# Products with v on four quarters of the array, two banks per product, in an attention + feed-forward kernel

## The chip, the cores and the metric

The kernel runs on one core of a Trainium2 chip. The metric is the device time of one execution in microseconds (us). TensorE (PE) multiplies matrices and writes to PSUM banks; VectorE (DVE) and ScalarE (ACT) work on data in SBUF and PSUM; GpSimd (POOL) works on SBUF alone; SyncE (SP) issues the DMAs. The engines run their instructions in program order and wait for each other by semaphores.

## The reference

Attention over a window of 128 positions for 8 batches of 8 heads (576 positions, 64 values a head), and behind it two big products with a nonlinear step between them:

```python
scores = scale * np.matmul(q, k.transpose(0, 1, 3, 2))
mask = (rel >= 0) & (rel < window)
scores = np.where(mask, scores + bias[None], -1000000000.0)
attn = np.exp(scores - max) / (sum + 1e-09)
x = np.matmul(attn, v)             # 4608 tokens x 512 after reordering
h = x @ w_in                       # 512 -> 2048
g = h * erf(softplus(h))
return g @ w_out                   # 2048 -> 512
```

## The kernel before

**Attention** is cut into 48 spans, numbered n = 0 to 47: twelve chunks c of 384 tokens, and for each of them four pairs g of heads (j = 0, 1 in a pair). Two of three chunks are of a first kind (`w` = 0, one batch, 32 spans in all); the third is of a second kind (`w` = 1, the rest of two batches, 16 spans). Each span runs through these steps:

- `scores`: 64x64 matmuls q k^T into two PSUM banks, one for each head j. Head j lies on partitions 64 j and up, so it uses one half of the array's rows; the two halves of the queries use one half of its columns each. A matmul uses one quarter of the array. In the second kind the three tiles are done as a group of two and a group of one.
- `softmax`: DVE adds the bias table and takes the minimum (line 470), ACT takes the exponentials (line 478).
- `normalise`: DVE inverts the sums; POOL (in the first four spans also DVE) scales the probabilities p (line 501).
- `transpose_bank`: PE transposes p by blocks of 128 (line 521) into a bank `t`, and DVE or ACT copies it to `pa`, two or three banks for each span. After the transpose the two heads lie beside each other.
- `av`: px = v^T p^T on the whole array (line 537), 6 matmuls of 64 to 192 columns in the first kind and 10 in the second, all into one bank. v lies in memory with zeros for the other head, so that the two heads don't mix. From span 8 on px shares the bank `t` with the transposes.
- DVE or ACT copies px to `xs` (or, in the first two chunks, straight to `xr`), and SP stores it.

**The feed-forward part** takes x by chunks. Everything is done in split precision: a value is held as a high and a low part, and each product is three matmuls. Line 732 makes h, line 714 or 718 (ACT or DVE) copies it out, lines 769 and 771 are softplus and erf on ACT, lines 781 and 785 are DVE's, and line 803 makes o. The first pass does 7 of the 16 slices of w_in and w_out for all tokens (h blocks of 384 columns) and runs interleaved with attention; the second pass does the other 9 (blocks of 512) and begins when attention has ended and its SBUF is free. Each slice of the weights is prepared by ACT and DVE (lines 608 to 629).

**Order.** Nothing is reordered on the chip. `Plan.run` lists all steps with the buffers that they read and write and their planned costs, and places them one after another: on each free engine the ready step with the smallest due time `at` goes first, if its buffers are free. A step that lists several engines takes the one that can have it first. Pools give the number of buffers: banks `s` 2, `t` 1, `h` 2, three for o; `TB`, `PB`, `VB` are those of pa, p and v. In the first 8 spans (`SPARE`) the banks of o and h, not yet in use, serve attention too.

Of the kernel before, what the change touches and what calls it, by code (L numbers as in the profile page):

```python
# [18 lines left out]
NPAIR = H // 2  # L19
# [21 lines left out]
MB, KH, KS = 15, 4, 2  # L41
PB, XB, OB, TB = 8, 3, 3, 4
QB, VB = 4, 2
# [15 lines left out]
TILES = [  # L59
    [(2, 128), (3, 0), (3, 0)],  # L60
    [(3, 0), (3, 0), (3, 0)],
]
QUERIES = [(128, 0, 640), (0, 128, 256)]
PIECES = [[(128, 384)], [(0, 128), (384, 512)], [(512, 768)]]
KEYS = [
# [6 lines left out]
]  # L72
GROUPS = [[(0, 1, 2)], [(0, 1), (2,)]]
BANKS = [
# [5 lines left out]
]  # L80
VALUES = [
# [6 lines left out]
]  # L88
SUB = ALU.subtract

# [251 lines left out]
class Attention:  # L342


    def __init__(self, tc, plan, ctx, actx, qk, vb, bias, ident, moe):
# [26 lines left out]
        self.step = self.n = 0  # L372
        self.loaded = []
        for c in range(3 * B // 2):
            for g in range(NPAIR):
                self.span(c, g)
                self.n += 1

# [26 lines left out]
    def values(self, c, g, w, at):  # L405

        v = Buf(self.vp, [P, 10, P], F32, "v", VB, f"v{self.n}")
        blocks = 10 if w else 6
        self.plan.op(emit=lambda e: self.nc.sync.dma_start(v[:, :blocks], self.src_v[c, g, :, :blocks]), w=[v], at=at,
                     **dma(P * blocks * P * 4))  # L410
        return v
# [9 lines left out]
    def scores(self, w, x, ready, at):  # L421
# [5 lines left out]
        for group in groups:  # L427
# [31 lines left out]
    def softmax(self, g, w, t, ps, low, total, at):  # L459
        nc, op = self.nc, self.plan.op  # L460
        blocks, c0 = TILES[w][t]
        n = 64 * blocks
        nm = f"{self.n}_{t}"
        pt = Buf(self.pp, [P, 3, 2, 64], F32, "p", PB, f"p{nm}")
        cut = lambda x: x.rearrange("p (c d) -> p c d", d=64)
        table = self.tables[g]

        def biased(e):
            for j in range(2):
                nc.vector.tensor_tensor_reduce(  # L470
                    out=pt[:, :blocks, j, :], in0=cut(ps[j].all), in1=cut(table.ap[:, j * 256 + c0 : j * 256 + c0 + n]),
                    scale=-0.125, scalar=3.0e38, op0=ALU.add, op1=ALU.min, accum_out=low[:, j : j + 1],
                )
# [9 lines left out]
        return pt  # L483

    def normalise(self, w, p, st, totals, at):
# [9 lines left out]
        for t in range(3):  # L495
            blocks = TILES[w][t][0]

            def scaled(e, t=t, blocks=blocks):
                for j in range(2):
                    dst = p[t][:, :blocks, j, :]  # L500
                    (nc.vector if e == "DVE" else nc.gpsimd).tensor_scalar(  # L501
# [7 lines left out]
    def transpose_bank(self, w, bi, p, sb, at):  # L509
        nc, op = self.nc, self.plan.op  # L510
        parts, c0, c1 = BANKS[w][bi]
        nm = f"t{self.n}_{bi}"
# [5 lines left out]
        def transposes(e):  # L518
            cut = ps[:, :].rearrange("p (c d) -> p c d", d=64)
            for n, (t, kb, a, b) in enumerate(parts):  # L520
# [7 lines left out]
        op({"DVE": dve(c1 - c0), "Act": act(c1 - c0, src=0.06)},  # L528
           lambda e: self.copy(e, sb[bi][:, : c1 - c0], ps[:, c0:c1]), r=[ps], w=[sb[bi]], at=at)

    def av(self, w, step, dst, v, sb, at):
        todo = VALUES[w][step]
        last = step == len(VALUES[w]) - 1
# [8 lines left out]
        self.plan.op({"PE": sum(fp32_us(x[-1]) for x in todo) + 0.015}, products,  # L542
                     r=[v, *(sb[x] for x in sorted({y[1] for y in todo}))], w=[dst], at=at)

    def span(self, c, g):
        op, n = self.plan.op, self.n
        w = int(c % 3 == 2)
# [6 lines left out]
        for t in range(3):  # L554
# [4 lines left out]
            self.step += 1  # L559
        self.normalise(w, p, st, totals, at)  # L560
        at += LT
        sb = [Buf(self.ptp, [P, 512], F32, "pa", TB, f"pa{n}_{x}") for x in range(len(BANKS[w]))]
        for bi in range(len(BANKS[w])):
            self.transpose_bank(w, bi, p, sb, at)
# [12 lines left out]
        self.moe.x_parts[c].append(xd)  # L577
        op(emit=lambda e: self.nc.sync.dma_start(xd.all, xs.all), r=[xs], w=[xd],
           at=at + 0.1, **dma(P * CH * 4))
# [312 lines left out]
def _layout(q, k, v, moe_w_in, moe_w_out):  # L892
# [7 lines left out]
    qk = np.zeros((nc, NPAIR, 2, D, 1024), q.dtype)  # L900
    vb = np.zeros((nc, NPAIR, 2, 64, 10, 2, D), v.dtype)
    for c in range(nc):
# [5 lines left out]
        else:  # L908
            order = [(qh, x, 6), (qh, x, 7), (qh, y, 6), (qh, y, 7), (qh, x, 8), (qh, y, 8)]
            order += [(kh, b, n) for b in (x, y) for n in range(4, 9)]  # L910
            values = [(b, kb) for b in (x, y) for kb in range(4, 9)]
        for n, (src, b, block) in enumerate(order):
            qk[c, :, :, :, n * 64 : n * 64 + 64] = src[b, :, :, :, block]
        for n, (b, kb) in enumerate(values):
            for j in range(2):
                vb[c, :, j, :, n, j] = vh[b, :, j, kb]
    bits = lambda a: a.view(np.int64)
# [4 lines left out]
    rel = np.concatenate([  # L922
        np.where(low, r + 128, r - 64) - col, r + 64 - col, r - col, np.where(low, -1, r - 64 - col),
    ], axis=1)
    bias = np.where((rel >= 0) & (rel < WIN), -4.0 * rel, -1e30)
    bias = np.concatenate([bias, bias / 2], axis=1).astype(np.float32)
    return {
        "qk": qk.reshape(nc, NPAIR, P, 1024), "v_b": vb.reshape(nc, NPAIR, P, 10, P), "w_in": wi.reshape(NF, P, DM),
        "w_out": wo.reshape(NF, P, DM), "bias": bias,
# [19 lines left out]
```

## Time and profile before

| | |
|---|---|
| median of 3 runs | 1029.47 us (1029.36 to 1030.06) |
| the profiled execution | 1029.15 us, of which its span is 1027.4 us |
| PE busy | 1013.1 us, 99% of the span |
| ACT, DVE, POOL busy | 640.3, 543.2, 132.7 us |
| granted clock of PE | 0.999 of full speed (2.4 GHz) over the span |
| scores, transposes, px in time | from 3.9 to 437 us, interleaved with the first pass |
| second pass | from 567 us on |

The profile comes from one execution; its span runs from the first to the last instruction. Busy times of PE include the pipeline's tail of each matmul, so the distance from one start to the next tells more than a duration. A matmul of float32 data leaves two records.

### The profile page before, as it was taken

To read this page: it belongs to the slowest core of one execution; us is meant where nothing else is said; L and a number is where in the kernel's file an instruction comes from. 1 tells how busy PE (TensorE), PEld (TensorE's weight loads), DVE (VectorE), ACT (ScalarE), POOL (GpSimd) and SP (SyncE) were. 2 spreads that over 40 slices of the span, in tenths; PEclk is the share of its full clock that TensorE was granted. 3 is DMA by queue.
4 is the path that set the end of the run, shared out by engine and by line. 5 is a ranking of instruction groups with operands and counts; after the bars stand their busy time and mean duration, and the time that the engine had idled before them with its cause. 6 is when DMAs were issued, how large, how long until landed. Compare 5 with 4: busy or idle time off the path is not lost.

```text
span 1027.4 us, 17078 instructions
## 1 busy us (share of the span) xinstructions
PE 1013.1 (99%) x6468; PEld 868.6 (85%) x6468; DVE 543.2 (53%) x1343; ACT 640.3 (62%) x1308; POOL 132.7 (13%) x274
## 2 busy tenths in 40 slices
PE   8999999999999999999999999999999999999998
PEld 7888988888888888898988888888888888888886
DVE  6999854635544645376437944435353534435252
ACT  6989875766865775677668854535454453544452
POOL 0633422223203313100000100000000000000000
PEclk9999999999999999999999999999999999999999
DMA  8777563545353553164103420303031212212011
GB/s 291 234 277 244 160 227 99 176 121 173 119 176 102 162 145 129 42 203 144 62 17 97 134 87 16 123 1 123 2 122 38 86 53 71 82 42 82 0 62 41
DMA packets 52993, 117.23 MB, mean 114 GB/s; under 512 B 5168, under 2 KB 21552, under 8 KB 52912
## 3 DMA queue, kind: packets, MB, share of 16 engines
q1 hardware_dynamic: 52912, 116.15, 34.8%
q8 instruction: 51, 0.84, 0.3%
q14 instruction: 30, 0.25, 0.1%
HBM read 87.82 MB, written 28.31 MB: 113 GB/s over the span
## 4 chain that ended last, share of the span: by engine, by line
PE 87%; ACT 6%; DVE 3%; DMA 2%; issue 1%; POOL 0%; SPq 0%; ACTq 0%; DVEq 0%
PE o L803 37%; PE h L732 35%; PE px L537 7%; PE s L448 4%; PE t L521 4%; ACT p L478 1%; DMA wri<-w_in 1%; ACT pa L415 1%; DMA wro<-w_out 1%; ACT s L769 1%; ACT s L771 0%; POOL p L501 0%; DMA qk<-qk 0%; DMA xd<-xr 0%; ACT L771 0%
## 5 line engine op out<-in xcount | busy, mean ns | idle before, releaser
L732 PE MATMUL h<-xh,whi 128*128 128x384 f32 (+1 forms) x660 | 244.4, 370 | 0.3 <-ACT hs L714 0.3
L732 PE MATMUL h<-xh,wli 128*128 128x384 f32 (+1 forms) x660 | 239.5, 363 | 0.0
L732 PE MATMUL h<-xl,whi 128*128 128x384 f32 (+1 forms) x660 | 239.0, 362 | 0.0
L803 PE MATMUL o<-who,gh 128*128 128x512 f32 x576 | 230.8, 401 | 0.2
L803 PE MATMUL o<-who,gl 128*128 128x512 f32 x576 | 225.6, 392 | 0.0
L803 PE MATMUL o<-wlo,gh 128*128 128x512 f32 x576 | 225.2, 391 | 0.0
L714 ACT COPY hs<-h 128x384 f32<-128x384 f32 (+2 forms) x132 | 60.4, 468 | 241.0 <-PE h L732 240.9
L501 POOL TENSOR_SCALAR p<-p,st 128x192 f32<-128x192 f32 (+1 forms) x264 | 127.2, 501 | 300.1 <-DVE st L492 230.1
L732 PEld LDWEIGHTS h<-xh,whi 128*128 128x128 f32 x660 | 124.1, 188 | 17.8 <-issue 1.7
L732 PEld LDWEIGHTS h<-xl,whi 128*128 128x128 f32 x660 | 124.1, 188 | 14.8
L478 ACT ACTIVATE p<-p,st 128x192 f32<-128x192 f32 (+1 forms) x288 | 124.4, 437 | 17.7 <-DVE st L470 17.5
L732 PEld LDWEIGHTS h<-xh,wli 128*128 128x128 f32 x660 | 123.8, 188 | 12.6
L718 DVE COPY hs<-h 128x512 f32<-128x512 f32 (+2 forms) x61 | 35.3, 579 | 179.8 <-PE h L732 162.2
L803 PEld LDWEIGHTS o<-who,gl 128*128 128x128 f32 x576 | 108.1, 188 | 23.0
L803 PEld LDWEIGHTS o<-who,gh 128*128 128x128 f32 x576 | 108.3, 188 | 22.1 <-issue 2.1
L470 DVE CUSTOM_DVE_ANT_0 p<-s,tables 128x192 f32<-128x192 f32 (+1 forms) x288 | 82.6, 337 | 82.0 <-PE s L448 77.1
L803 PEld LDWEIGHTS o<-wlo,gh 128*128 128x128 f32 x576 | 108.4, 188 | 18.8
L537 PEld LDWEIGHTS px<-pa,v 128*128 128x128 f32 x704 | 99.9, 191 | 8.5 <-ACT pa L415 4.6
L537 PE MATMUL px<-pa,v 128*128 128x192 f32 (+2 forms) x704 | 103.2, 299 | 2.2 <-ACT pa L415 1.1
L781 DVE TENSOR_TENSOR hs<-s,hs 128x768 f32<-128x768 f32 (+1 forms) x106 | 90.2, 886 | 21.4 <-ACT s L771 21.4
L785 DVE TENSOR_TENSOR gl<-hs,gh 128x768 fp32r<-128x768 f32 (+1 forms) x106 | 90.9, 885 | 6.1 <-ACT gh L714 5.3
L769 ACT ACTIVATE s<-hs 128x768 f32<-128x768 f32 (+1 forms) x106 | 76.4, 776 | 0.5
(58 smaller groups left out, 976.7 us busy)
## 6 DMA issues: line engine op xcount, KB each, us to landing
v<-v_b SPq DMA_DIRECT2D x32, 384.0 KB, 3.7
xr<-xd SPq DMA_DIRECT2D x16, 768.0 KB, 4.9
qk<-qk SPq DMA_DIRECT2D x30, 384.0 KB, 3.8
v<-v_b SPq DMA_DIRECT2D x16, 640.0 KB, 4.5
pd<-ot SPq DMA_DIRECT2D x36, 256.0 KB, 4.2
ot<-pd SPq DMA_DIRECT2D x36, 256.0 KB, 3.4
wri<-w_in SPq DMA_DIRECT2D x16, 512.0 KB, 4.3
qk<-qk SPq DMA_DIRECT2D x16, 512.0 KB, 4.8
```

The lines of the kernel that those rows point to most:

```text
L448: nc.tensor.matmul(part[j].all[rows, 64 * to : 64 * (to + n)], lhsT=x[d, q0 + 64 * half : q0 + 64 * half + 64], rhs=x[d, k0 : k0 + 64 * n] ...
L470: nc.vector.tensor_tensor_reduce(out=pt[:, :blocks, j, :], in0=cut(ps[j].all), in1=cut(table.ap[:, j * 256 + c0 : j * 256 + c0 + n]), scal ...
L478: nc.scalar.activation(dst, dst, AF.Exp, bias=low[:, j : j + 1], scale=-1.0, accum_out=total[:, j : j + 1])
L501: (nc.vector if e == "DVE" else nc.gpsimd).tensor_scalar(dst, dst, totals[t][:, j : j + 1], 1.0, op0=ALU.mult, op1=ALU.mult)
L521: nc.tensor.matmul(cut[:, a : b + 1 : b - a], lhsT=p[t][:, kb].rearrange("p j d -> p (j d)"), rhs=self.ident[:, :], is_transpose=True, sta ...
L537: self.nc.tensor.matmul(dst[:, to : to + size], lhsT=v[:, blk], rhs=sb[s][:, off : off + size], start=(step + n == 0), stop=(last and n == ...
L714: self.nc.scalar.copy(out, src)
L732: nc.tensor.matmul(ps[:, :W], lhsT=ww[:, cs], rhs=xx[:, k], start=(k2 + k + n == 0), stop=(k2 + k + n == 4),)
L769: A.activation(s[:, :n], hs[:, :n], AF.Softplus)
L781: op({"DVE": dve(n)}, lambda e, s=s, hs=hs, n=n: V.tensor_tensor(hs[:, :n], s[:, :n], hs[:, :n], ALU.mult), r=[s, hs], w=[hs], at=at)
L785: op({"DVE": dve(n)}, lambda e, gh=gh, gl=gl, hs=hs, n=n: V.tensor_tensor(gl[:, :n], hs[:, :n], gh[:, :n], SUB), r=[hs, gh], w=[gl], at=at)
L803: nc.tensor.matmul(po.all, lhsT=gg[:, cs], rhs=w.all, start=(u["start"] and n == 0), stop=(u["end"] and n == 2),)
```

## The change

The products with v are done on the four quarters of the array. After the transposes a quarter takes 64 keys (its rows: upper or lower partitions of `pa`) and one head j (its columns: the half of px's partitions). The keys on the upper rows add up in one bank, those on the lower rows in another, and so ACT copies the first bank to `xs` and DVE then adds the second to it, in every span. v holds no zeros any more (384 or 704 columns for each span instead of 768 or 1280). For each block of 64 keys the head that the transpose puts on the upper rows is now chosen by a table (`SLOTS`, `FIRST`), so that all four quarters get about the same number of columns: 8 blocks of 64 each in the first kind; 8, 10, 10 and 8 in the second. From span 8 on the two banks are the two `s` banks of the scores; before that they are two spare banks of o. `pa` is one buffer of 1152 columns, filled from banks of 512 (first kind, two) or 384 (second kind, three).

The scores' keys are cut so that each half of each tile has exactly two segments, issued in turn over the four quarters: 24 matmuls a span, where it was 16 or 18. The steps up to `normalise` of a span (`weights`) are now listed ahead of the transposes and products of the span before (`apply`).

```diff
-PB, XB, OB, TB = 8, 3, 3, 4
+PB, XB, OB, TB = 8, 3, 3, 2
...
         for c in range(3 * B // 2):
             for g in range(NPAIR):
-                self.span(c, g)
-                self.n += 1
+                state = self.n, c, g, *self.weights(c, g)
+                if last:
+                    self.apply(*last)
+                last = state
+                self.n = state[0] + 1
+        self.apply(*last)
...
-                    for half, segments in enumerate(KEYS[w][t]):
-                        rows = slice(64 * half, 64 * half + 64)
-                        for k0, to, n in segments:
+                    for k in range(2):
+                        for half, segments in enumerate(KEYS[w][t]):
+                            rows = slice(64 * half, 64 * half + 64)
+                            k0, to, n = segments[k]
...
-                    dst = pt[:, :blocks, j, :]
+                    dst = pt[:, own[j], :]
...
-                    cut[:, a : b + 1 : b - a], lhsT=p[t][:, kb].rearrange("p j d -> p (j d)"),
+                    cut[:, a : b + 1 : b - a], lhsT=p[t][:, 2 * k : 2 * k + 2].rearrange("p j d -> p (j d)"),
...
+    def av(self, w, dst, v, sb, parts, at):
+
+        left = {k: list(x) for k, x in VALUES[w].items()}
+        spent = dict.fromkeys(left, 0)
+        todo = []
+        while left:
+            k = min(left, key=lambda k: (spent[k], k))
+            todo.append((*k, *left[k].pop(0), not spent[k], len(left[k]) == 0))
+            spent[k] += todo[-1][5]
+            if not left[k]:
+                del left[k]
 
         def products(e):
-            for n, (blk, s, off, to, size) in enumerate(todo):
+            for pos, j, blk, slot, q, n, first, last in todo:
+                rows = slice(64 * pos, 64 * pos + 64)
                 self.nc.tensor.matmul(
-                    dst[:, to : to + size], lhsT=v[:, blk], rhs=sb[s][:, off : off + size],
-                    start=(step + n == 0), stop=(last and n == len(todo) - 1),
+                    dst[pos][64 * j : 64 * j + 64, 64 * q : 64 * (q + n)], lhsT=v[rows, 64 * blk : 64 * blk + 64],
+                    rhs=sb[rows, 64 * slot : 64 * (slot + n)], start=first, stop=last,
                 )
...
-        pool, tag = (self.spare[1], "o0") if n < SPARE else (self.ps, "t")
-        px = Buf(pool, [P, 512], F32, tag, 1, f"px{n}")
-        for step in range(len(VALUES[w])):
-            self.av(w, step, px, v, sb, at + 0.1)
+        ways = [(self.spare[1], "o0", 1), (self.spare[1], "o2", 1)] if n < SPARE else [(self.ps, "s", 2)] * 2
+        px = [Buf(pool, [P, 512], F32, tag, bufs, f"px{n}_{k}") for k, (pool, tag, bufs) in enumerate(ways)]
+        self.av(w, px, v, sb, parts, at + 0.1)
...
-        op({"DVE": dve(CH), "Act": act(CH, src=0.06)},
-           lambda e: self.copy(e, xs.all, px[:, :CH]), r=[px], w=[xs], at=at + 0.1)
+        op({"Act": act(CH, src=0.06)}, lambda e: nc.scalar.copy(xs.all, px[0][:, :CH]), r=[px[0]], w=[xs], at=at + 0.1)
+        op({"DVE": dve(CH)}, lambda e: nc.vector.tensor_tensor(xs.all, px[1][:, :CH], xs.all, ALU.add),
+           r=[px[1], xs], w=[xs], at=at + 0.1)
```

The planner makes a new order of all engines from this. Two places of it follow; names carry the span's number (px12 is the product of span 12).

PE before, at the product of span 12, the first one after the first pass's weights are prepared:

```order
L732 MATMUL h9_1591<-xl1_1_1328,whi2_858 128x384
L732 MATMUL h9_1591<-xh1_1_1326,wli2_869 128x384
L537 MATMUL px12_1633<-pa12_0_1587,v12_1362 128x192 x2
L537 MATMUL px12_1633<-pa12_0_1587,v12_1362 128x128
L537 MATMUL px12_1633<-pa12_1_1625,v12_1362 128x192 x2
L537 MATMUL px12_1633<-pa12_1_1625,v12_1362 128x64
L803 MATMUL o0_0_1439<-who2_1339,gh2_1555 128x512
L803 MATMUL o0_0_1439<-wlo2_1344,gh2_1555 128x512
L803 MATMUL o0_0_1439<-who2_1339,gl2_1602 128x512
L448 MATMUL s15_0_0_1663<-qk15_1228 64x128
```

PE there now; px12_0 and px12_1 are the two banks, for the upper and the lower rows:

```order
L841 MATMUL o2_0_1609<-wlo3_1669,gh2_1548 128x512
L841 MATMUL o2_0_1609<-who3_1652,gl2_1708 128x512
L565 MATMUL px12_0_1872<-pa12_1837,v12_1524 64x192
L565 MATMUL px12_0_1872<-pa12_1837,v12_1524 64x128
L565 MATMUL px12_1_1875<-pa12_1837,v12_1524 64x192
L565 MATMUL px12_1_1875<-pa12_1837,v12_1524 64x128
L565 MATMUL px12_0_1872<-pa12_1837,v12_1524 64x64
L565 MATMUL px12_1_1875<-pa12_1837,v12_1524 64x192
L565 MATMUL px12_0_1872<-pa12_1837,v12_1524 64x64
L565 MATMUL px12_0_1872<-pa12_1837,v12_1524 64x192
L565 MATMUL px12_1_1875<-pa12_1837,v12_1524 64x192
L565 MATMUL px12_0_1872<-pa12_1837,v12_1524 64x128
```

Six whole-array matmuls into one bank have become 15 on quarters, into two banks in turn (the last five stand below these); a block of twelve h follows, where three o and the next scores stood.

DVE before, where it takes the result of that product out of PSUM:

```order
L470 ISA p14_2_1649,st14_1630<-s14_0_0_1566,tables_158 128x3x64
L470 ISA st14_1630 128x1
L470 ISA p14_2_1649,st14_1630<-s14_0_1_1568,tables_158 128x3x64
L470 ISA st14_1630 128x1
L419 COPY xs12_1661<-px12_1633 128x384
L781 TENSOR_TENSOR hs4_2_1238<-s4_1293,hs4_2_1238 128x384
L707 TENSOR_TENSOR xl2_0_1685<-xr2_1_1538,xh2_0_1637 128x768
```

DVE there now:

```order
L756 CAST gh4_1870<-hs4_2_1274 128x384
L823 TENSOR_TENSOR gl4_1889<-hs4_2_1274,gh4_1870 128x384
L756 CAST xh2_0_1891<-xr2_1_1813 128x768
L745 TENSOR_TENSOR xl2_0_1893<-xr2_1_1813,xh2_0_1891 128x768
L756 COPY hs10_0_1904<-h10_1830 128x384
L819 TENSOR_TENSOR hs5_0_1316<-s5_1815,hs5_0_1316 128x768
L612 TENSOR_TENSOR xs12_1906<-px12_1_1875,xs12_1906 128x384
L756 CAST gh5_1923<-hs5_0_1316 128x768
L823 TENSOR_TENSOR gl5_1952<-hs5_0_1316,gh5_1923 128x768
```

The copy from px has become an addition that also reads `xs12`, and stands behind six feed-forward steps; before, the copy stood right behind the bias steps of span 14.

ACT now, at the same place (before, it had no part in this product):

```order
L809 ACT_TABLE_LOAD
L809 ACTIVATE s5_1815<-s5_1815 128x768
L809 ACTIVATE s7_1817<-s7_1817 128x768
L809 ACTIVATE s9_1819<-s9_1819 128x384
L811 ACT_TABLE_LOAD
L611 COPY xs12_1906<-px12_0_1872 128x384
L492 ACTIVATE p13_1_1854,st13_1792<-p13_1_1854,st13_1792 128x192 x2
```

ACT's copy of the first bank stands behind a whole group of softplus and erf with its table loads, and the exponentials of the next span behind it.

## Rows read from the trace of the kernel before

**Rows 1.** The page's busy line, and the lines of its chain:

```profile
PE 1013.1 (99%) x6468; PEld 868.6 (85%) x6468; DVE 543.2 (53%) x1343; ACT 640.3 (62%) x1308; POOL 132.7 (13%) x274
...
PE 87%; ACT 6%; DVE 3%; DMA 2%; issue 1%; POOL 0%; SPq 0%; ACTq 0%; DVEq 0%
PE o L803 37%; PE h L732 35%; PE px L537 7%; PE s L448 4%; PE t L521 4%; ACT p L478 1%; DMA wri<-w_in 1%; ACT pa L415 1%; DMA wro<-w_out 1%; ACT s L769 1%; ACT s L771 0%; POOL p L501 0%; DMA qk<-qk 0%; DMA xd<-xr 0%; ACT L771 0%
```

**Rows 2.** Busy time of the engines by stretch of the span (x instructions):

```profile
core 0: us, PE busy (x) PEld busy (x) DVE busy (x) ACT busy (x) POOL busy (x), PEclk, DMA share, GB/s
25.00:50.00 25.00, 23.91 (x261) 21.90 (x260) 23.52 (x93) 22.94 (x81) 14.69 (x28) 1.00 0.76 241
...
75.00:100.00 25.00, 23.34 (x216) 20.49 (x206) 23.55 (x63) 24.39 (x56) 8.95 (x12) 1.00 0.73 251
125.00:275.00 150.00, 149.97 (x1294) 131.24 (x1293) 75.67 (x280) 103.79 (x281) 39.24 (x90) 1.00 0.48 153
...
440.00:567.00 127.00, 126.58 (x632) 113.78 (x632) 79.11 (x120) 93.09 (x133) 1.20 (x1) 1.00 0.33 105
```

**Rows 3.** Timeline of PE, a product of the first kind: start, us, what:

```profile
150.09 1.85 PE L537 MATMUL px<-pa,v 128*128 128x192 f32 x12
151.75 0.42 PE L732 MATMUL h<-xh,whi 128*128 128x384 f32 x1
152.01 0.34 PE L732 MATMUL h<-xl,whi 128*128 128x384 f32 x1
152.18 0.34 PE L732 MATMUL h<-xh,wli 128*128 128x384 f32 x1
```

**Rows 4.** Timeline of PE, a product of the second kind and scores behind it:

```profile
174.34 2.60 PE L537 MATMUL px<-pa,v 128*128 128x192 f32 x20
176.87 0.90 PE L448 MATMUL s<-qk 64*64 64x192 f32 x24
```

**Rows 5.** Timeline of PE, blocks of scores between feed-forward products:

```profile
156.10 0.90 PE L448 MATMUL s<-qk 64*64 64x192 f32 x24
156.93 0.44 PE L732 MATMUL h<-xh,whi 128*128 128x384 f32 x1
...
199.43 0.34 PE L732 MATMUL h<-xh,wli 128*128 128x384 f32 x1
199.70 1.12 PE L448 MATMUL s<-qk 64*64 64x128 f32 x32
200.75 0.50 PE L803 MATMUL o<-who,gh 128*128 128x512 f32 x1
201.09 0.39 PE L803 MATMUL o<-wlo,gh 128*128 128x512 f32 x1
201.32 0.40 PE L803 MATMUL o<-who,gl 128*128 128x512 f32 x1
```

**Rows 6.** Timeline of PE, the stretch 199.695 to 199.725 alone:

```profile
199.70 0.34 PE L448 MATMUL s<-qk 64*64 64x128 f32 x4
```

**Rows 7.** Timelines of PE and DVE, the product of span 12 and its copy:

```profile
100.78 1.96 PE L537 MATMUL px<-pa,v 128*128 128x192 f32 x12
...
102.78 0.56 DVE L419 COPY xs<-px 128x384 f32<-128x384 f32 x1 [0.61 <-PE px L537]
```

**Rows 8.** Groups by line and shape, DVE and ACT: xcount | busy us, mean ns:

```profile
L825 DVE TENSOR_TENSOR ot<-o,ot 128x512 f32<-128x512 f32 x36 | 24.6, 692 | 45.7 <-PE o L803 45.6
...
L419 DVE COPY pa<-t 128x512 f32<-128x512 f32 x16 | 11.0, 690 | 15.8 <-PE t L521 15.8
...
L419 DVE COPY xs<-px 128x384 f32<-128x384 f32 x18 | 10.0, 556 | 11.6 <-PE px L537 9.4 <-ACT p L478 1.6
...
L415 ACT COPY xs<-px 128x384 f32<-128x384 f32 x22 | 10.5, 477 | 28.9 <-PE px L537 28.8
```

**Rows 9.** Waits, 25 to 125 us, then the whole span: us, times, longest:

```profile
PEld t L521 <- ACT pa L415: 2.9, 5, 0.9
...
PE s L448 <- DMA qk<-qk: 2.6, 3, 1.2
```

More of the change, by code (lines that the diff above doesn't have):

```diff
@@ L59 @@
 TILES = [
-    [(2, 128), (3, 0), (3, 0)],
-    [(3, 0), (3, 0), (3, 0)],
+    [(2, 0), (3, 64), (3, 64)],
+    [(3, 64), (3, 64), (3, 64)],
+]
+SLOTS = [
+    [((0, 3), (1, 1)), ((0, 1), (3, 1)), ((3, 1), (0, 1))],
+    [((0, 1), (3, 1)), ((3, 1), (0, 1)), ((3, 1), (0, 1))],
 ]
@@ L373, in __init__ @@
         self.loaded = []
+        last = None
         for c in range(3 * B // 2):
             for g in range(NPAIR):
-                self.span(c, g)
-                self.n += 1
+                state = self.n, c, g, *self.weights(c, g)
[4 more added lines that the diff above has]
+        self.apply(*last)
     def warm_up(self):
@@ L405, in values @@
     def values(self, c, g, w, at):
[L407 to L410, printed above, removed]
+        v = Buf(self.vp, [P, 704], F32, "v", VB, f"v{self.n}")
+        size = 704 if w else 384
+        self.plan.op(emit=lambda e: self.nc.sync.dma_start(v[:, :size], self.src_v[c, g, :, :size]), w=[v], at=at,
+                     **dma(P * size * 4))
         return v
@@ L470, in biased @@
                 nc.vector.tensor_tensor_reduce(
-                    out=pt[:, :blocks, j, :], in0=cut(ps[j].all), in1=cut(table.ap[:, j * 256 + c0 : j * 256 + c0 + n]),
+                    out=pt[:, own[j], :], in0=cut(ps[j].all), in1=cut(table.ap[:, j * 256 + c0 : j * 256 + c0 + n]),
                     scale=-0.125, scalar=3.0e38, op0=ALU.add, op1=ALU.min, accum_out=low[:, j : j + 1],
@@ L483, in softmax, with slots @@
         return pt
+    def slots(self, w, t):
+        blocks = TILES[w][t][0]
+        return [slice(s, s + step * (blocks - 1) + 1, step) for s, step in SLOTS[w][t]]
     def normalise(self, w, p, st, totals, at):
@@ L496, in normalise, with scaled @@
             blocks = TILES[w][t][0]
-            def scaled(e, t=t, blocks=blocks):
+            def scaled(e, t=t, own=self.slots(w, t)):
                 for j in range(2):
-                    dst = p[t][:, :blocks, j, :]
+                    dst = p[t][:, own[j], :]
                     (nc.vector if e == "DVE" else nc.gpsimd).tensor_scalar(
@@ L510, in transpose_bank @@
         nc, op = self.nc, self.plan.op
-        parts, c0, c1 = BANKS[w][bi]
+        parts, size = BANKS[w][bi]
         nm = f"t{self.n}_{bi}"
@@ L519, in transposes @@
             cut = ps[:, :].rearrange("p (c d) -> p c d", d=64)
-            for n, (t, kb, a, b) in enumerate(parts):
+            for t, k, a, b in parts:
                 nc.tensor.matmul(
-                    cut[:, a : b + 1 : b - a], lhsT=p[t][:, kb].rearrange("p j d -> p (j d)"),
+                    cut[:, a : b + 1 : b - a], lhsT=p[t][:, 2 * k : 2 * k + 2].rearrange("p j d -> p (j d)"),
                     rhs=self.ident[:, :], is_transpose=True, start=True, stop=True,
@@ L527, in transpose_bank, with weights @@
            r=[p[t] for t in sorted({x[0] for x in parts})], w=[ps], at=at)
[L528 to L533, printed above, removed]
+        op({"DVE": dve(size), "Act": act(size, src=0.06)},
+           lambda e: self.copy(e, sb.all, ps[:, :size]), r=[ps], w=[sb], at=at)
+    def av(self, w, dst, v, sb, parts, at):
[8 more added lines that the diff above has]
+                del left[k]
         def products(e):
-            for n, (blk, s, off, to, size) in enumerate(todo):
+            for pos, j, blk, slot, q, n, first, last in todo:
+                rows = slice(64 * pos, 64 * pos + 64)
                 self.nc.tensor.matmul(
-                    dst[:, to : to + size], lhsT=v[:, blk], rhs=sb[s][:, off : off + size],
-                    start=(step + n == 0), stop=(last and n == len(todo) - 1),
-                )
[L542 to L546, printed above, removed]
+                    dst[pos][64 * j : 64 * j + 64, 64 * q : 64 * (q + n)], lhsT=v[rows, 64 * blk : 64 * blk + 64],
+                    rhs=sb[rows, 64 * slot : 64 * (slot + n)], start=first, stop=last,
+                )
+        self.plan.op({"PE": TURN + max(spent.values()) * 64 / 600.0 + 0.01 * len(todo)}, products,
+                     r=[v, *parts], w=dst, at=at)
+    def weights(self, c, g):
+        n = self.n
         w = int(c % 3 == 2)
@@ L560, in span, with apply @@
         self.normalise(w, p, st, totals, at)
+        return w, v, p, at
+    def apply(self, n, c, g, w, v, p, at):
+        op, nc = self.plan.op, self.nc
+        self.n = n
         at += LT
-        sb = [Buf(self.ptp, [P, 512], F32, "pa", TB, f"pa{n}_{x}") for x in range(len(BANKS[w]))]
-        for bi in range(len(BANKS[w])):
-            self.transpose_bank(w, bi, p, sb, at)
-        pool, tag = (self.spare[1], "o0") if n < SPARE else (self.ps, "t")
-        px = Buf(pool, [P, 512], F32, tag, 1, f"px{n}")
-        for step in range(len(VALUES[w])):
-            self.av(w, step, px, v, sb, at + 0.1)
+        sb = Buf(self.ptp, [P, 1152], F32, "pa", TB, f"pa{n}")
+        parts, pos = [], 0
+        for bi, (_, size) in enumerate(BANKS[w]):
+            parts.append(Part(sb, slice(None), slice(pos, pos + size)))
+            self.transpose_bank(w, bi, p, parts[-1], at)
+            pos += size
+        ways = [(self.spare[1], "o0", 1), (self.spare[1], "o2", 1)] if n < SPARE else [(self.ps, "s", 2)] * 2
+        px = [Buf(pool, [P, 512], F32, tag, bufs, f"px{n}_{k}") for k, (pool, tag, bufs) in enumerate(ways)]
+        self.av(w, px, v, sb, parts, at + 0.1)
         if c < DIRECT:
@@ L910, in _layout @@
             order += [(kh, b, n) for b in (x, y) for n in range(4, 9)]
-            values = [(b, kb) for b in (x, y) for kb in range(4, 9)]
+            values = [*((b, kb) for b in (x, y) for kb in range(4, 9)), (y, 7)]
         for n, (src, b, block) in enumerate(order):
@@ L922, in _layout @@
     rel = np.concatenate([
-        np.where(low, r + 128, r - 64) - col, r + 64 - col, r - col, np.where(low, -1, r - 64 - col),
+        np.where(low, -1, r - 64 - col), r - col, np.where(low, r + 128, r - 64) - col, r + 64 - col,
     ], axis=1)
```

12 lines of the change are left out of this document (7 added, 5 removed), and 36 rows, old and new, of tables (BANKS, KEYS, VALUES).

## The prediction

> **What bounds the kernel now.** I read the page's busy line and its chain first. TensorE (PE) is busy for 1013 of 1027.4 us, and the chain runs on it for 87%: the two big products of the second half (o, h) take 72%, the product with v (px, line 537) 7%, scores 4%, transposes 4% [rows 1]. The reader should see that the span is the sum of PE's work plus a little idle time. The table by stretch then says where that little is [rows 2]: in the stretches from 25 to 50 and from 75 to 100 us VectorE (DVE) and ScalarE (ACT) are busy for 23 to 24 of 25 us, and PE is the engine that waits (1.1 and 1.7 us of 25 are empty even by its overlapping records), most of all for copies of transposes [rows 9]. After 125 us PE is full and DVE is busy for half, ACT for two thirds. So a microsecond of PE work saved after 125 us should come off the span, and one saved before 100 us should not.
>
> **What the change takes off PE.** Prices are start to start, with what the block makes slow beside it. A product of the first kind (32 of the 48 spans) starts at 150.09 and ends at 151.75, and the first h after it takes 0.26 us where the next takes 0.17: 1.66 + 0.09 = 1.75 us [rows 3]. The second kind (16 spans) takes 2.53 us up to a block of scores [rows 4]. Of these 0.10 is the entry into scores (the last h before a block starts at 199.43 and should be done by 199.60; the block starts at 199.70 [rows 5]), which leaves 2.43.
>
> What the new form costs no row shows for px, but scores already run on four quarters, with the same split: rows of the array give the bank, columns the half of the partitions. Their block of 16 matmuls (32 records) has 512 columns on each quarter and takes 1.05 us, the 384-column block 0.83 [rows 5]. The new product of the first kind has 15 matmuls and 8 blocks of 64 = 512 columns on each quarter: 1.05. The second kind has 22 matmuls and at most 10 blocks = 640 columns: 1.05 + 0.22 = 1.27, by the step between the two rows. Each block pays 0.10 to enter, and 0.11 in the first o behind it (0.34 where the next takes 0.23 [rows 5]). So 1.26 for 1.75, and 1.48 for 2.43: 32 x 0.49 + 16 x 0.95 = 15.7 + 15.2 = **30.9 us**. Both ends of this: nothing saved if the quarters didn't overlap (against it stand the 1.05 us, in which one quarter alone would do a fourth of the columns), 32 if the five places where the order now puts scores and products side by side save an entry and an exit each.
>
> Scores keep their columns (512 a quarter) but go from 16 to 24 matmuls in the first kind and from 18 to 24 in the second. Does a matmul cost, or a column? Four records of a block start within 0.02 us of each other [rows 6], so the start of one holds up the others little, and I take columns: no cost. The Trainium skill ("TensorE: Matmul & The Clock Gate", Part 1, on the 56 ns gap) says that starts never come closer than about 25 ns, however small the product. By that, 48 records would need 1.2 us where the block has 1.05, and the sum below would be 4.8 us higher; the row with four starts in 0.02 us speaks against it [rows 6]. Transposes stay 400, in 104 runs as before.
>
> **What it adds beside PE.** The copy of px out of PSUM (ACT 0.48 or DVE 0.56 us) becomes an ACT copy and a DVE addition for every span. An addition that reads PSUM costs what a copy does (0.692 against 0.690 for 512 columns), so 0.56 [rows 8]. Before, DVE did 20 of the 48 and ACT 28; now each has 48: 28 x 0.56 = 16 us more on DVE, 20 x 0.48 = 10 us more on ACT. Copies of transposes grow from 448 to 512 columns on one of two banks. After 125 us these lie under engines that are busy for half and two thirds [rows 2]; I cost them at nothing there, and if that cover were gone they would cost up to their 16 us.
>
> Before 100 us there is no cover. I take one place, the product of span 12, the first after the first pass's weights: it starts at 100.78, and DVE copies it at 102.78 behind a full queue [rows 7]. By the order, ahead of that copy DVE had 4 copies of products and 5 of transposes; now it has 12 additions and 11 copies: 8 x 0.56 + 6 x 0.69 = 8.6 us [rows 8]. The rest of its queue nets to +0.4 (two more hs, one more gl, xl and gh, less one span of scores). So the place comes 9 us later; ACT's queue up to its copy for span 11 has grown from 120 to 132 instructions, about 7 us, so ACT has no room to take it over. PE in the meantime has ahead of that product 12 more h (2.0) and 18 more o (4.1), one span of scores less (1.26), and twelve cheaper products (8 x 0.49 + 4 x 0.95 = 7.7): 2.9 us less. It reaches the place with 2.9 us less work and finds it 9 us later: nearly **12 us more idle**. PE's next scores write the banks that the product used, so they wait for that addition. I take 11, since PE idles a little there already. Ends: 0, if planner and engines shift other work into the gap, and 16, if ACT's 7 us and DVE's 9 add up.
>
> **Smaller edits.** v shrinks to half in memory: PE waited 2.6 us for qk in all and never for v [rows 9], so 0, at best -2. Store and prefetch keep their queue; the store waits for the addition, half a microsecond later, with the next loads behind it, which are needed microseconds later: 0. Attention ends later in the program: between the last product and the second pass PE now has 56 us of work instead of 131, and in it DVE must prepare that pass's weights and its first x, some 46 us by the order. It fits: 0, at worst +5.
>
> **Sum.** The profiled execution took 1029.15 us, 1.75 above its span; the median of the runs is 0.3 higher. 1029.15 - 30.9 + 11 = 1009.3, and on the median's footing 1009.5. I say **1009 us**, 2% faster.
>
> **Rivals.**
> Full gain: PE's 30.9 us come through, because the early queue finds other work for PE. For it: the order has moved 6 us of h and o up there. Against it: those need ACT and DVE too. 1029.5 - 30.9 = 998.6.
> Banks: from span 8 on each product takes both banks of the scores and holds them until ACT has copied one and DVE has added the other. Idle engines need 0.04 + 0.48 + 0.56 (from product end to copy 0.04 [rows 7]) and the steps between; the order puts some 2 us of PE work there. But ACT's copy stands behind whole groups of table loads and softplus, as the order shows at span 12. If each of 40 spans waits 0.3 us more than planned, +12: 1021.
> Matmuls, not columns: if what sets a block's length is its records (1.05 / 32 = 0.033 us each), the 64-column pieces cost as much as large ones. Scores gain 16 records in each of 32 spans and 12 in each of 16, 704 x 0.033 = 23 us; the 44 records of a product of the second kind make 1.45 instead of 1.27, +3. 1009 + 26 = 1035, slower than before. It decides where a record costs about 0.03 us: there the 26 us shrink to the 20 that are left of the gain. The rows that time blocks can't tell records from columns, since both grow together; the four starts in 0.02 us speak against it [rows 6].
> A milder form: small pieces cost something between the two, and a scores block of 48 records takes 1.20 instead of 1.05. 32 x 0.15 = 4.8: 1014. This is where the rule of the Trainium skill named above would lead.
>
> **How the numbers follow.** Forecast (1003 to 1015) 0.56, the milder form 0.05, full gain 0.15, banks 0.16, matmuls 0.08. The range goes to 997 for the full gain and to 1021, the middle of the banks case; what it leaves out is that case's upper half and the matmuls. Slower by over 0.2%, about what a measurement of this kernel can tell from no change, is most of the matmuls case: 0.06; within 0.2%: 0.03; faster: 0.91.
>
> **What would show it.** Right: px blocks of about 1.05 and 1.27 us, scores still 1.05 and 0.83; at the product of span 12 a start near 110 us; PE full from 125 us on. Wrong: blocks of scores near 1.5 us (matmuls), waits of scores on xs all through the stretch from 125 us on (banks), or span 12 near 100 us (full gain). A DVE or ACT that stays above 90% busy after 150 us would break the sum too, and so would a second pass that waits for its weights.

## The result and the profile after

The changed kernel takes 1011.23 us (median of 4 runs, 1010.40 to 1012.89); before took 1029.41 us beside it. The ratio is 0.982, with a 95% interval from 0.981 to 0.984. The forecast was 1009 us, between 997 and 1021. The profiled execution, the slowest of the four, took 1012.89 us, 16.3 less than that of before (1029.15); by the medians the change gains 18.2.

The page's busy line of the kernel after, and rows by stretch (us, busy us of PE, PEld, DVE, ACT and POOL, PE's granted clock, DMA share, GB/s) that answer to [rows 1, 2]:

```profile
PE 989.3 (98%) x8132; PEld 832.4 (82%) x8132; DVE 569.8 (56%) x1392; ACT 641.5 (63%) x1308; POOL 134.5 (13%) x273
```

```profile
25.00:50.00 25.00, 20.48 (x404) 16.58 (x403) 22.91 (x91) 23.18 (x82) 12.03 (x24) 0.93 0.62 190
...
75.00:100.00 25.00, 21.76 (x259) 17.14 (x257) 23.77 (x62) 22.68 (x53) 8.95 (x14) 0.93 0.51 172
100.00:125.00 25.00, 23.32 (x222) 19.79 (x222) 21.05 (x56) 19.55 (x46) 10.50 (x16) 0.93 0.48 150
125.00:275.00 150.00, 149.96 (x1785) 127.22 (x1784) 84.45 (x281) 109.64 (x280) 35.66 (x78) 1.00 0.38 124
...
440.00:567.00 127.00, 123.73 (x954) 106.26 (x954) 91.16 (x184) 95.73 (x173) 16.80 (x31) 1.00 0.38 129
```

PE is still full from 125 us on. Before that it now misses 4.5 us from 25 to 50 us and 3.2 from 75 to 100, where it missed 1.1 and 1.7, and DVE and ACT are busy for 22 to 24 of 25 us as before. The third column from the right holds something new: a granted clock of 0.93 in three of the early stretches, where it was 1.00 [rows 2].

A timeline of PE in the kernel after, one product of each kind and blocks of scores; they answer to [rows 3, 4, 5]:

```profile
159.54 1.13 PE L461 MATMUL s<-qk 64*64 64x64 f32 x48
160.60 0.50 PE L841 MATMUL o<-who,gh 128*128 128x512 f32 x1
...
187.65 0.34 PE L770 MATMUL h<-xh,wli 128*128 128x384 f32 x1
187.92 1.11 PE L565 MATMUL px<-pa,v 64*64 64x192 f32 x30
188.96 0.55 PE L540 MATMUL t<-ident,p 128*128 128x128 f32 x3
...
190.81 0.90 PE L461 MATMUL s<-qk 64*64 64x128 f32 x32
191.64 0.55 PE L540 MATMUL t<-ident,p 128*128 128x128 f32 x3
...
195.67 0.34 PE L770 MATMUL h<-xh,wli 128*128 128x384 f32 x1
195.94 1.33 PE L565 MATMUL px<-pa,v 64*64 64x192 f32 x44
197.21 0.44 PE L770 MATMUL h<-xh,whi 128*128 128x384 f32 x1
197.49 0.34 PE L770 MATMUL h<-xl,whi 128*128 128x384 f32 x1
```

Start to start, a product of the first kind takes 188.96 - 187.92 = 1.04 us (forecast 1.05) and one of the second 1.27 (forecast 1.27). The entry is 0.10 (the h at 195.67 should be done at 195.84, the product starts at 195.94), the exit 0.11 (the h at 197.21 takes 0.28 where the next takes 0.17). Scores take 1.06 us in 48 records where they took 1.05 in 32, and 0.83 as before, there in 32 records instead of 24. So here columns set the time, not the number of matmuls.

### The profile page after: what moved, and what is told of

Its sections match the earlier page's. It is cut to its first block, busy times and chain, and to the rows that moved or that the text cites. A ratio compares the mean times of both kernels' runs of the same rounds, so it can differ in the third digit from the quotient of the medians.

```text
span 1011.1 us, 20445 instructions
## 1 busy us (share of the span) xinstructions
PE 989.3 (98%) x8132; PEld 832.4 (82%) x8132; DVE 569.8 (56%) x1392; ACT 641.5 (63%) x1308; POOL 134.5 (13%) x273
## 3 DMA queue, kind: packets, MB, share of 16 engines
q8 instruction: 64, 1.05, 0.4%
## 5 line engine op out<-in xcount | busy, mean ns | idle before, releaser
L770 PE MATMUL h<-xh,whi 128*128 128x384 f32 (+1 forms) x660 | 246.9, 374 | 1.0 <-ACT hs L752 1.0
L752 ACT COPY hs<-h 128x384 f32<-128x384 f32 (+2 forms) x127 | 57.8, 467 | 210.4 <-PE h L770 210.2
L520 POOL TENSOR_SCALAR p<-p,st 128x192 f32<-128x192 f32 (+1 forms) x264 | 130.2, 512 | 351.9 <-DVE st L511 217.7
L756 DVE COPY hs<-h 128x512 f32<-128x512 f32 (+2 forms) x66 | 38.1, 577 | 162.8 <-PE h L770 145.5
L841 PEld LDWEIGHTS o<-who,gh 128*128 128x128 f32 x576 | 108.5, 188 | 23.4 <-DVE ot L756 1.5
L809 ACT ACTIVATE s<-s 128x768 f32<-128x768 f32 (+1 forms) x106 | 76.5, 776 | 0.5
L461 PEld LDWEIGHTS s<-qk 64*64 64x64 f32 x2304 | 56.0, 139 | 23.8 <-issue 9.3
```

The costliest lines, as they stand in the source:

```text
L461: nc.tensor.matmul(part[j].all[rows, 64 * to : 64 * (to + n)], lhsT=x[d, q0 + 64 * half : q0 + 64 * half + 64], rhs=x[d, k0 : k0 + 64 * n] ...
L520: (nc.vector if e == "DVE" else nc.gpsimd).tensor_scalar(dst, dst, totals[t][:, j : j + 1], 1.0, op0=ALU.mult, op1=ALU.mult)
L752: self.nc.scalar.copy(out, src)
L756: self.nc.vector.tensor_copy(out, src)
L770: nc.tensor.matmul(ps[:, :W], lhsT=ww[:, cs], rhs=xx[:, k], start=(k2 + k + n == 0), stop=(k2 + k + n == 4),)
L809: A.activation(s[:, :n], s[:, :n], AF.Erf)
```

## The experiments

**Where PE is the bound, and where it isn't.** The products of twelve early spans, and in another kernel of twelve later ones, were issued twice: the same extra work for PE at two places, with the order of everything else unchanged.

```diff
+        times = 2 if 0 <= self.n < 12 else 1      # the other kernel: 24 <= self.n < 36
...
-            for pos, j, blk, slot, q, n, first, last in todo:
+            for pos, j, blk, slot, q, n, first, last in todo * times:
```

> The products of spans 0 to 11 are issued twice, 8 x 1.04 + 4 x 1.26 = 13.4 us more of TensorE's work, all of it before 110 us; nothing else changes. Theory (in the early stage VectorE and ScalarE set the pace, and TensorE idles about 15 us there): less than half of it is seen, +0 to +6 us on the kernel after. Rival (TensorE bounds there too, and the 12 us between the full gain and the measured one are lost elsewhere): +11 to +14 us.

> The products of spans 24 to 35 are issued twice, the same 13.4 us of TensorE's work, but in the stretch from 125 us on. Theory (TensorE is full there): +12 to +14 us on the kernel after. Rival (the blocks hide waits, on the banks or on copies, there too): +0 to +8 us.

Measured: 1016.14 us (+4.9 on the kernel after) for the early ones, 1020.29 (+9.1) for the late ones, which lies in neither range forecast for them (12 to 14, and 0 to 8). A second product right behind the first costs less than I took. The block of 60 records in the kernel with late doubles:

```profile
257.24 1.99 PE L566 MATMUL px<-pa,v 64*64 64x192 f32 x60
259.16 0.44 PE L771 MATMUL h<-xh,whi 128*128 128x384 f32 x1
```

That is 1.92 instead of 1.04, and of the second kind 2.38 instead of 1.26, so the real addition is 8 x 0.88 + 4 x 1.11 = 11.5 us. Late, the trace shows nearly all of it: from the product of span 22 (at 216.25 us) to the end of the last matmul 796.4 us, in the kernel after (from 221.26) 785.1, so 11.3 more. The whole times of these two executions differ by less, 6.4 us, because the one with late doubles reached span 22 some 5 us sooner, ahead of any doubled product; how that can be, stands in the next experiment but one. Early, less than half is seen, also when the start of the first product, which differs between executions, is left out: from there to the product of span 13 it takes 103.79 us with the early doubles, 102.69 in the kernel after and 99.67 in the kernel with late doubles, whose order is the same up to there. That is 1.1 or 4.1 of 11.5 us. So PE is the bound from 125 us on, and ahead of that mostly not.

**What holds PE up early.** DVE's addition was cut to 8 of its 384 columns in spans 0 to 13, which leaves most of the second bank out of x there; the order stays.

```diff
-        op({"DVE": dve(CH)}, lambda e: nc.vector.tensor_tensor(xs.all, px[1][:, :CH], xs.all, ALU.add),
+        cut = 8 if n < 14 else CH
+        op({"DVE": dve(CH)}, lambda e: nc.vector.tensor_tensor(xs.all[:, :cut], px[1][:, :cut], xs.all[:, :cut], ALU.add),
```

> VectorE's addition takes 8 of its 384 columns for spans 0 to 13, so most of the sum over the second bank is left out there; the order of all instructions stays. 14 additions of 0.55 us become some of about 0.1 us, 6 us less of VectorE's work before 125 us. Theory (VectorE's queue sets the early stage, and the added work on it is what held back the product of span 12): 3 to 8 us faster than the kernel after, and that product starts 3 to 7 us before 108.4. Rival (ScalarE's copies, or its groups of table loads, set the stage): 0 to 1.5 us faster.

The first eight additions, in the kernel after and with the cut (line, engine, count, shortest/median/longest in ns, first and last start):

```profile
L612 DVE TENSOR_TENSOR xr<-px,xr x8: 539/556/558, 26.7 to 55.7; 128x384 f32<-128x384 f32 x8
```

```profile
L613 DVE TENSOR_TENSOR xr<-px,xr x8: 147/161/167, 25.8 to 52.5; 128x8 f32<-128x8 f32 x8
```

Measured: 1006.71 us, 4.5 faster than after. 14 additions lost 0.40 us each, 5.5 us of DVE's work, and the time fell by 4.5. The product of span 12 starts at 104.40 instead of 108.41. Counted from the start of the first product, it comes after 81.42 us, where it took 85.04 in the kernel after and 85.08 in the one with late doubles: 3.6 us sooner, for 12 additions ahead of it that lost 4.8. So work added to DVE there costs about three quarters of its length; the prediction had taken the 9 us in full. DVE isn't alone: of PE's waits from 25 to 125 us, 3.0 us in the kernel after and 3.4 with the cut are for ACT's copies of the first bank, and no run takes these off ACT alone.

**A clock that fell behind a wait of PE.** This needs no kernel of its own: ahead of span 24 the kernel with late doubles runs the same instructions in the same order as the kernel after. PE from the product of span 12 on, first in the kernel after, then there:

```profile
108.41 1.21 PE L565 MATMUL px<-pa,v 64*64 64x192 f32 x30
...
114.54 1.25 PE L461 MATMUL s<-qk 64*64 64x64 f32 x46 [1.68 <-DVE xs L612]
...
116.31 0.63 PE L841 MATMUL o<-wlo,gh 128*128 128x512 f32 x1
116.74 0.63 PE L841 MATMUL o<-who,gl 128*128 128x512 f32 x1
...
126.06 1.11 PE L565 MATMUL px<-pa,v 64*64 64x192 f32 x30
```

```profile
106.50 1.21 PE L566 MATMUL px<-pa,v 64*64 64x192 f32 x30
...
111.09 1.12 PE L461 MATMUL s<-qk 64*64 64x64 f32 x46 [0.15 <-DVE xs L613]
...
112.49 0.39 PE L842 MATMUL o<-wlo,gh 128*128 128x512 f32 x1
112.72 0.40 PE L842 MATMUL o<-who,gl 128*128 128x512 f32 x1
...
121.09 1.11 PE L566 MATMUL px<-pa,v 64*64 64x192 f32 x30
```

In the first the scores wait 1.68 us for DVE's addition, and behind that wait o's stand 0.43 apart instead of 0.23: the clock has fallen to its lower level, 1.2 GHz. In the second the wait is 0.15 and the clock stays. What made the wait long is one step earlier: DVE waits for the load of x for the feed-forward part (the same row, kernel after, then the other):

```profile
111.13 0.56 DVE L756 CAST xh<-xr 128x768 fp32r<-128x768 f32 x1 [1.79 <-DMA xr<-xd]
```

```profile
107.69 0.56 DVE L757 CAST xh<-xr 128x768 fp32r<-128x768 f32 x1 [0.26 <-DMA xr<-xd]
```

Counted from the product, the transfer landed 1.53 us later (it was issued 0.5 later and took 6.4 us instead of 5.3), and PE waited 1.53 us longer. From the product of span 12 to that of span 13 it is 126.06 - 108.41 = 17.65 us against 121.09 - 106.50 = 14.59: 3.06 us more. The kernel with the small additions tells the two costs apart: at the same place

```profile
110.11 1.12 PE L461 MATMUL s<-qk 64*64 64x64 f32 x46 [1.37 <-DVE xs L613]
```

PE waits 1.37 us, the granted clock stays 1.00, and from product to product it takes 120.10 - 104.40 = 15.70 us. There 1.22 us more of wait cost 1.11, about its own length; in the kernel after, the fallen clock doubled what the wait cost. What makes the clock fall, these runs don't settle: a wait of 1.55 us at this place, in the kernel of x5 below, left it at 1.00 as well.

A fallen clock needn't cost anything: some 30 us earlier it fell in the kernel after too and not in the one with late doubles,

```profile
80.50:83.50 3.00, 2.51 (x31) 1.77 (x34) 2.74 (x8) 2.97 (x6) 0.00 (x0) 0.63 0.47 137
```

```profile
79.00:82.00 3.00, 2.61 (x49) 2.02 (x50) 2.88 (x9) 2.97 (x7) 0.00 (x0) 1.00 0.37 122
```

(0.63 against 1.00, third column from the right), and from that product to the next it took 95.69 - 81.60 = 14.09 us in the one and 93.76 - 79.68 = 14.08 in the other. There DVE and ACT set the pace (they are busy for 2.7 to 3.0 of 3 us), and a slower PE only waited less: 0.4 us for the additions and copies ahead of its next scores, against 1.6. In the kernel with early doubles, where PE has more to do between its waits, the clock of all four early stretches is 1.00.

**The order of issue over the quarters.** The matmuls of a product were issued one quarter after the other, not in turn.

```diff
+        todo.sort(key=lambda x: x[:2])
```

> The 15 or 22 matmuls of a product are issued one quarter of the array after the other, instead of taking turns; work and result are the same. If the quarters overlap because neighbours in the order of issue go to different quarters: a block has 4 x 512 columns in a row with overlap only where the quarter changes, 2 to 3.4 us instead of 1.04, and the kernel is 45 to 100 us slower than after. If each quarter has a queue of its own that runs ahead whatever the order: 1.04 and 1.26 stay, and the time is that of after within 0.3%.

```profile
206.09 2.36 PE L566 MATMUL px<-pa,v 64*64 64x192 f32 x30
208.37 0.55 PE L540 MATMUL t<-ident,p 128*128 128x128 f32 x3
...
215.37 3.69 PE L566 MATMUL px<-pa,v 64*64 64x192 f32 x44
218.99 0.44 PE L771 MATMUL h<-xh,whi 128*128 128x384 f32 x1
```

Measured: 1078.95 us, 67.7 slower than after and 5% slower than before. A product takes 2.29 and 3.62 us instead of 1.04 and 1.26. 32 x 1.25 + 16 x 2.36 = 77.8 us of PE's work; 12 of these spans are early, and there some of it is hidden. Nothing but the order of issue differs, so the overlap of the quarters hangs on neighbours in that order going to different quarters. That the change takes turns (`min(left, ...)` in `av`) is what makes it a gain at all.

**The listing.** One part of the change alone was undone: the transposes and the product of a span are listed right behind its own weights again.

```diff
-                if last:
-                    self.apply(*last)
-                last = state
+                self.apply(*state)
...
-        self.apply(*last)
```

> Undoes one part of the change alone: a span's product is listed right behind its own weights again, not behind the weights of the next span. In the order that follows, VectorE's work ahead of an early addition less TensorE's work ahead of its product is at most 31 us (at span 10), where it is 39 us (at span 12) in the kernel after. Theory (this difference is TensorE's early idle time): 4 to 9 us faster than after. Rival (a product listed in turn waits for the copies of its own transposes, which the listing was to avoid): 48 waits of some 0.3 us, up to 15 us slower.

Measured: 1260.36 us, 249 slower than after and 22% slower than before (1.221 to 1.225). Neither the theory (4 to 9 faster) nor the rival (up to 15 slower) was near it. Busy times in one stretch, and PE's timeline from one product to the next:

```profile
125.00:275.00 150.00, 113.78 (x1110) 93.45 (x1110) 52.48 (x177) 73.14 (x181) 22.84 (x54) 0.83 0.24 80
```

```profile
529.49 1.96 PE L561 MATMUL px<-pa,v 64*64 64x192 f32 x44
532.02 0.43 PE L457 MATMUL s<-qk 64*64 64x128 f32 x2 [0.56 <-ACT xs L607]
532.61 0.89 PE L457 MATMUL s<-qk 64*64 64x128 f32 x30 [0.16 <-DVE xs L608]
534.71 0.83 PE L457 MATMUL s<-qk 64*64 64x128 f32 x16 [1.21 <-DVE st L480]
538.17 0.48 PE L536 MATMUL t<-ident,p 128*128 128x128 f32 x1 [2.62 <-POOL p L516]
...
543.12 3.04 PE L561 MATMUL px<-pa,v 64*64 64x192 f32 x44
```

The `s` banks are given out in the order of the list. Listed in turn, the next span's scores can't have them before this span's product has been copied and added, and that product needs this span's whole softmax. So 13.6 us pass here in a row: product, copy, addition, scores, exponentials, sums, GpSimd's scaling, transposes, copies, next product. From 125 to 275 us DVE and ACT are under half busy, and PE has its 76% at a mean clock of 0.83. By its waits from 125 to 800 us PE lost 52.2 us to GpSimd's scaling, 41.4 to DVE's xh (x for the feed-forward part comes late) and 23.4 to the copies and additions ahead of the scores. Listed one span later, the next span's scores come ahead of the product, and their softmax runs while the product waits. That it is the shared banks which make the listing matter is argued from the list and this stretch: a product listed in turn but with banks of its own wasn't tried, as all eight banks are taken; the kernel before is listed in turn, has its product in the bank `t` and doesn't stall.

**Three ways to take work off DVE early.** The copy of the first bank on either engine (x5); all early scalings of p on GpSimd instead of half on DVE (x7); both, with half of those scalings (x8).

```diff
-ND = 4
+ND = 0      # x7; 2 in x8, unchanged in x5
...
-        op({"Act": act(CH, src=0.06)}, lambda e: nc.scalar.copy(xs.all, px[0][:, :CH]), r=[px[0]], w=[xs], at=at + 0.1)
+        op({"DVE": dve(CH), "Act": act(CH, src=0.06)}, lambda e: self.copy(e, xs.all, px[0][:, :CH]), r=[px[0]], w=[xs], at=at + 0.1)      # x5, x8
```

> The copy of the product's first bank may go to VectorE or ScalarE, as the planner chooses; the planner then writes the order anew. Theory (VectorE's queue sets the early stage): VectorE's work ahead of each early addition is the same within 1 us of the kernel after, by its order, so 0 to 2 us either way. Rival (ScalarE's copies, stuck behind its groups of table loads and softplus, set it): 3 to 8 us faster than after.

> All scalings of probabilities go to GpSimd; in the kernel after, VectorE did 24 of them in the early spans at 0.3 us each, 7 us of its work before 125 us. In the order that follows the largest difference between VectorE's work ahead of an addition and TensorE's ahead of its product is 27 us instead of 39. Theory (VectorE's queue sets the early stage): 5 to 11 us faster than after. Rival (the slower scaling on GpSimd, 0.51 us for one, becomes the early bound): 0 to 5 us slower.

> Half of VectorE's early scalings stay, half go to GpSimd, and the copy of the product's first bank may go to VectorE or ScalarE. The largest difference between VectorE's work ahead of an addition and TensorE's ahead of its product is 22 us by the new order, the smallest of all versions (39 in the kernel after). Theory: 8 to 14 us faster than after, about 1000 us. Rival (ScalarE or the loads set the early stage): within 3 us of after.

Measured: 1009.50 (x5), 1005.14 (x7) and 1006.36 us (x8); 1.7, 6.1 and 4.9 faster than after. x5 and x7 lie in the theory's ranges, with x7's ratio to before between 0.974 and 0.978. But x5 says little about its rival: of the 13 first-bank copies ahead of 110 us the planner gave DVE only one, so ACT's copies as the early bound stay untested. And x7's order is new throughout: no wait of PE for an addition is listed there from 25 to 125 us, so its 6.1 us needn't be the scalings alone. x8's 4.9 us fits neither the theory (8 to 14) nor its rival (within 3). For x8 I had counted wrong: where a product stands in two pieces in the order, I had taken the pieces for two spans. With products counted whole its largest difference is 31 us, not 22 (the 39 of after and 27 of x7 hold), and 8 us less than in after would be some 1003; this count was made after the result was known.

**Further in that direction.** In x7's kernel the first big product is made due earlier, by 8 and by 16 us.

```diff
-ND = 4
+ND = 0
-MC, MP, MH = 0.01, 16, -16
+MC, MP, MH = 0.01, 16, -24      # -32 in x10
```

> All scalings on GpSimd, as in the run before that was fastest (1005 us), and the first big product due 8 us earlier by the planner, which then writes the order anew. By that order TensorE's priced work is 967 us (971 in the kernel after and with the scalings alone: fewer changes between kinds of work) and the largest difference between VectorE's work ahead of an addition and TensorE's ahead of its product is 24 us (39 after, 27 with the scalings alone). Theory (early idle time is that difference): 4 to 8 us faster than with the scalings alone, 997 to 1001 us. Rival (with VectorE relieved, ScalarE or the loads set the early stage): 1003 to 1008 us.

> The same with the first big product due 16 us earlier: 967 us of priced work and a largest difference of 25 us. Theory: 997 to 1001 us. Rival: 1003 to 1008 us.

Measured: 1003.72 (x9; 0.973 to 0.976 of before) and 1011.71 us (x10). x9 is the fastest kernel here, 7.5 us faster than the change, but not to be told apart from x7. Both miss the theory (997 to 1001); x9 lies where its rival put it (1003 to 1008, with ACT or the loads as the early bound), and in it DVE waits 4.2 us for one load of x. So the difference between the two queues no longer tells the time. About half of what x10 loses against x9, it loses between the last product and the second pass. That stretch in x9 and in x10:

```profile
500.00:560.00 60.00, 59.19 (x319) 50.06 (x318) 51.11 (x78) 48.56 (x68) 5.02 (x4) 1.00 0.49 165
```

```profile
500.00:560.00 60.00, 55.36 (x332) 46.48 (x331) 47.36 (x74) 42.72 (x62) 4.52 (x6) 0.97 0.45 155
```

PE misses 0.8 us in the first and 4.6 in the second, there mostly for `xl` and `hs` from DVE (2.0 and 1.6 us). The other half is early: up to 125 us PE misses 14.7 us in x10 and 10.6 in x9, though the difference between the queues is nearly the same (25 and 24 us).

## Why the prediction was right

**The products on PE, -30.9 us: right.** Blocks of 1.04 and 1.27 us with 0.10 and 0.11 around them agree with the 1.26 and 1.48 of the sum. By these prices and the order, PE's work is 1001.9 us before and 971.0 after. The late doubles show that such work counts fully from 125 us on.

**Scores, 0: right.** 48 records take 1.06 us. This ends the matmuls rival (nearly 1.5 us) and the milder one (1.20), and with the latter the rule of the Trainium skill ("TensorE: Matmul & The Clock Gate", Part 1) as I had read it, by which 48 starts take 1.2 us.

**The early stage, +11: the mechanism right up to span 12.** The product of span 12 starts at 108.41 (forecast: near 110) with 77.7 us of priced work ahead of it, so 30.7 us late; before it was 100.78 and 81.3, 19.5 us. That is 11.2 us more idle time. (By the prediction's own 2.9 us less work it would be 10.5.) DVE was busy for 96.8 us ahead of its addition there, and for 88.4 ahead of its copy before: 8.4 us more, where the prediction counted 9.

**The store and the next loads, 0: the step that failed.** By the end of the profiled execution the two kernels differ by 14.7 us (1006.4 less 971.0 is 35.4; 1022.6 less 1001.9 is 20.7), and 3.6 of this came at once, between span 12 and span 13: the wait for one load and the fallen clock behind it, 3.06 us, shown above. The prediction said: "Store and prefetch keep their queue; the store waits for the addition, half a microsecond later, with the next loads behind it, which are needed microseconds later: 0." SyncE's issues from the store of span 11 to the load of x that reads it back, before and then after:

```profile
91.06 0.33 SPq L578 DMA_DIRECT2D xd<-xs  x1
92.19 0.33 SPq L600 DMA_DIRECT2D wri<-w_in  x1
94.27 0.33 SPq L695 DMA_DIRECT2D xr<-xd  x1
```

```profile
99.44 0.39 SPq L616 DMA_DIRECT2D xd<-xs  x1
101.17 0.33 SPq L411 DMA_DIRECT2D qk<-qk  x1
102.90 0.33 SPq L638 DMA_DIRECT2D wri<-w_in  x1
104.75 0.33 SPq L733 DMA_DIRECT2D xr<-xd  x1
```

The half microsecond held: the store goes out 3.75 us behind the start of its product (95.69), where it was 3.57 (87.49). But the queue's order isn't kept: one more transfer (qk) stands between store and load, and the load goes out 5.3 us behind the store instead of 3.2 and lands 6.4 us later instead of 5.6. Nor was there time to spare: before, ACT took what the load brought 0.7 us after it landed; now DVE waits for it, ahead of the addition that PE's next scores need, for 1.79 us, and with the same early order for 1.30 and 0.26 in the kernels with early and late doubles and for 2.02 in the one with small additions. The prediction put the clock at nothing, too. By the medians (18.2 us gained of 30.9) all losses together are 12.7, not 14.7: how much of this an execution pays differs.

**The second pass, 0 to +5: within its bounds, but not 0.** From 440 to 567 us PE misses 3.3 of 127 us, where it missed 0.4 [rows 2], so 2.9 more: 2.2 us of it in two waits of o for gl from DVE, 1.1 in one for ot. x10 shows the upper end, 4.6. The losses don't add up by these prices: 11.2, 3.6 and 2.9 make 17.7 us where 14.7 are seen. So 3 us came back that no run here assigns; the prices of PE's work may be off by as much. That the total fell so near the forecast is in part luck: two terms put at 0 measured 3.6 and 2.9, and nearly half of that doesn't show in the total.

**Copies late, 0: right.** DVE and ACT stay at 56 and 73% from 125 to 275 us. Of PE's waits from 125 to 550 us one row is listed (us in all, times, longest):

```profile
PE o L841 <- DVE gl L823: 1.3, 1, 1.3
```

**The banks: not met, for a reason that I hadn't priced.** The rival had 0.3 us for each span. In the kernel after no scores wait for xs after 125 us. But without the listing it is 249 us, 5 for each span. The prediction named the listing and gave it no price; no row of the kernel before could have shown what it is worth.

## What to carry to other kernels

Small matmuls on quarters of the array cost what the columns of the fullest quarter cost if neighbours in the order of issue go to different quarters (1.04 and 1.26 us here), and twice to three times that if they don't (2.29 and 3.62). When buffers that are given out in order get a second use, the list must put the next round's first use ahead of it, or everything between the two runs in series. And where another engine sets the pace of a stretch, price what is added to that engine at most of its length (three quarters here), and follow it through stores and loads back to that engine: a wait of PE at the end of that way cost its own length, and twice that in the execution in which the clock fell.

## What the hardware showed beyond that

- Behind a wait of 1.7 us the granted clock fell to its lower level, and it came back while PE was busy (third column from the right, then 1.00 from 120 us on). Behind waits of 1.37 and 1.55 us at the same place, in other kernels, it didn't fall. It fell twice earlier in that execution, and in none of the early stretches of the kernel before [rows 2].

```profile
114.80:117.80 3.00, 3.00 (x51) 2.50 (x41) 2.93 (x17) 1.82 (x8) 1.36 (x4) 0.60 0.48 155
```

- Two executions of the same early order reached span 13 at 126.06 and 121.09 us. 1.95 of these 5 us were there at the first product (23.37 and 21.42), 3.06 are the wait and the clock. So a difference of 2 us, and in single executions of 5, between kernels that differ elsewhere may be the early stage alone.
- Two products in a row overlap where they meet: the second costs 0.88 us where one alone takes 1.04.
